# Moving an activation table load, two k and q requests and four value loads in a fused attention and feed-forward kernel

## The chip, the cores and the metric

The kernel runs on one core of a Trainium2 chip. The metric is the device time of one execution in microseconds: the median of 3 runs before the change is 313.27 us (313.2 to 313.47).

The core has five engines with instruction streams of their own. PE (TensorE) multiplies matrices into PSUM. ACT (ScalarE) evaluates functions (exp, ln, silu) from a table that must be loaded, and copies. DVE (VectorE) does elementwise work and 32x32 transposes. POOL (GpSimd) does elementwise work and issues DMAs through a queue of its own ("software_dynamic", q0); its DMAs can convert fp32 to bf16 on the way. SP (SyncE) only issues DMAs ("hardware_dynamic", q1), without conversion. All DMAs share the same 16 DMA engines. An engine runs its instructions in the order in which they were written and waits at semaphores.

## The reference

Two steps. First attention over q, k, v of shape 8 batches x 8 heads x 576 positions x 64, in fp32, as the sum of two parts:

```
q_d, k_d, v_d = means over groups of 4 neighbouring positions      # 144 positions
out_up    = each row of softmax(q_d k_d^T / 8) v_d, repeated 4 times
out_local = softmax(q k^T / 8 where |i - j| < 4) v
x = out_up + out_local, as 4608 tokens x 512
```

Then a feed-forward part on all tokens: `h = x @ w_in` (512 to 2048), `g = h * sigmoid(1.702 h)`, `out = g @ w_out` (2048 to 512), in fp32.

## The kernel before, in words

**Groups and batches.** The feed-forward part goes in nine groups g of 512 tokens. Group g has `mm1` (L831: 16 blocks ffc of 128 hidden columns, each with four matmuls of L816 over the 512 inputs, then one silu on ACT, L827, into `gT`) and `mm2` (L857: 64 matmuls of L894 that read `gT` and `w_out_bf`, then four output copies `osb` on ACT, L879, and four stores on SP, L884). Batch 0's attention runs ahead of everything. The attention of batch b = g + 1 is woven into group g: the lists `POS` and `POS_0` (L923) name matmul counts at which a piece of `attention(b)` is put into PE's stream. In group 0 the pieces for batch 1 are two scores pieces (16 and 28; their exponentials at 18), four pieces `avx1`, one for each pair of heads (40, 49, 58, 67), and `prep_vd_pe(1)` at 36 (L388), which forms the means of batch 1's values on PE from `vb`.

**What one piece needs.** k and q of a batch come by `load_qk` (L218, POOL, bf16) in two halves qd, and are transposed on DVE (L311) into `kT`, `qT`. The sums over four positions are `kdT`, `qdT` (L330 on DVE, or L342 and L346 on POOL). The values come in five chunks of 128 rows, in two halves of 64 partitions each: for batch 1 by POOL's DMAs straight into the bf16 tile `vb` (`load_vb`, L249, ten DMAs); for later batches by SP's DMAs into the fp32 tile `vf` (`load_v`, L238, ten DMAs), which POOL then casts into `vb` (`prep_v`, L352). The means of the values for batches from 2 on come from a second fp32 copy `v4` (`load_v4`, L271, SP), which POOL sums in three steps kc (`prep_v4`, L359 and L362) into `vd`.

**avx1** (L597, batch 1) and **avx** (L671, later batches) multiply the exponentials with the values on PE. ACT takes ln of the sums and exp(-ln) (L638, L649), DVE copies and multiplies (L643, L656) into `xT`, and POOL or, for the last pair, DVE adds the upsampled part (L667). After the last pair's exponential L653 loads the silu table again, and the output copies of group 0 follow on ACT.

**Order of the requests.** The order is written by hand (`manual_schedule`). At the start POOL issues k and q of batch 0 (L218), five value loads (L259), three loads of `w_in_bf` (L281), k and q of batch 1, and quarters 1 and 2 of `w_out_bf` (L290). In the loop for g = 0 (L1044) come ten `load_vb` for batch 1, quarters 3 and 4 of `w_out_bf`, the preparation of batch 1's k and q on DVE with the requests for batch 2's, a memset of `v4` (L1055) and `load_v(2)`. POOL has eight DMA semaphores that it uses in turn, so each of its DMAs waits until the one eight places before it has landed. `load_v(b, gate)` takes an optional gate: a copy of one element of another tile into element `[0, chunk 0]` of the `vf` tile (`after`, L928; L930 in the profile). SP's loads of batch 2 come behind such a copy from quarter 4 of `w_out_bf`. The tile `vf` has one buffer.

In the loop for g = 1 (b = 2) the order on POOL is: sums of k and q, `prep_v(2)`, `prep_v4(2)` with its three steps, then the four requests for batch 3's k and q.

Of the kernel before, what the change touches and what calls it, by code (L numbers as in the profile page):

```python
# [19 lines left out]
def kernel(  # L20
# [9 lines left out]
    nc = tc.nc  # L30
# [320 lines left out]
        cp = eng.copy if eng is nc.scalar else eng.tensor_copy  # L351
        cp(out=vbs[b % 2][:, i, h, 0:D], in_=vf[b][:, i, h])  # L352

    def prep_v4(b, eng):
        for kc in range(3):
            x = v4[0:112, kc].rearrange("p h (f d) -> p h f d", f=4)
            t1 = work.tile([128, SD * 4], FP32, name="pq", tag="pq")
            t1 = t1[:, 0 : HP * 2 * D].rearrange("p (h f d) -> p h f d", h=HP, f=2)
            eng.tensor_tensor(  # L359
                out=t1[0:112], in0=x[:, :, 0:2, :], in1=x[:, :, 2:4, :], op=ALU.add  # L360
            )
            eng.tensor_tensor(  # L362
                out=vds[b % 2][0:112, kc, :, 0:D],
                in0=t1[0:112, :, 0, :], in1=t1[0:112, :, 1, :], op=ALU.add,
            )
# [231 lines left out]
    def avx1(b, hp):  # L597
        vb, vd = vbs[b % 2], vds[b % 2]
        T, u, m, L, W = PB[1:3], hp % 2, hp // 2, 300, 300 + SD

        def down(kc, den):
            rows = slice(64 * u, 64 * u + 48)
            for j in range(2):
                nc.tensor.matmul(
                    T[u][64 * j : 64 * j + 64, den, L:W],
                    lhsT=ones[rows, 1, :] if den else vd[rows, kc, 2 * m + j, 0:D],
                    rhs=eds[m][rows, j, SD * kc : SD * kc + SD],
                    start=(kc == 0), stop=(kc == 2),
                    tile_position=(64 * u, 64 * j),
                )  # L610

        def local(par, i=None):
            rows = slice(64 * par, 64 * par + 64)
            at = slice(0, L) if i is None else slice(60 * i, 60 * i + 60)
            for j in range(2):
                nc.tensor.matmul(
                    T[par][64 * j : 64 * j + 64, int(i is None), at],
                    lhsT=ones[rows, 0, :] if i is None else vb[rows, i, 2 * hp + j, 0:D],
                    rhs=es[hp][rows, j, at],
                    start=True, stop=True,  # L620
                    tile_position=(64 * par, 64 * j),
                )

        others = [0, 1, 2, 3, 4, None]
        for kc in range(3):
            for den in range(2):
                down(kc, den)
                local(1 - u, others[2 * kc + den])
        for i in others:
            local(u, i)  # L630

        l = work.tile([128, 2 * (S + SD)], FP32, name="l", tag="l", bufs=2)
        n = work.tile([128, 2 * (S + SD)], FP32, name="n", tag="n", bufs=1)
        od = work.tile([128, 2, SD], FP32, name="od", tag="od", bufs=2)[:, 0]
        part = [slice(0, W), slice(W, W + L)]

        def ln(x):
            nc.scalar.activation(  # L638
                out=l[:, part[x]], in_=T[x ^ u][:, 1, 0 : (W, L)[x]], func=AF.Ln
            )  # L640

        def copy(x):
            nc.vector.tensor_copy(out=n[:, part[x]], in_=T[x ^ u][:, 0, 0 : (W, L)[x]])  # L643

        ln(0)
        copy(1)
        ln(1)
        copy(0)
        nc.scalar.activation(  # L649
            out=l[:, 0 : W + L], in_=l[:, 0 : W + L], func=AF.Exp, scale=-1.0  # L650
        )
        if hp == HP - 1:
            nc.scalar.preload_act_table_set("silu_and_others")  # L653

        def mult(out, *part):
            nc.vector.tensor_tensor(out=out, in0=sub(n, *part), in1=sub(l, *part), op=ALU.mult)  # L656

        x, t0 = xT[hp], b * S
        at = (0, W) if u == 0 else (W, 0)
        mult(od, L, (1, SD))  # L660
        mult(sub(x, t0 + 3, (114, 5), (1, 57)), at[0] + 3, (60, 5), (1, 57))
        mult(sub(x, t0 + 60, (114, 5), (1, 57)), at[1], (60, 5), (1, 57))
        mult(sub(x, t0, (1, 3)), at[0], (1, 3))
        mult(sub(x, t0 + 573, (1, 3)), at[1] + 297, (1, 3))
        xs = x[:, t0 : t0 + S].rearrange("p (t f) -> p t f", f=4)
        eng = nc.vector if hp == HP - 1 else nc.gpsimd
        eng.tensor_tensor(out=xs, in0=xs, in1=sub(od, 0, (1, SD), (0, 4)), op=ALU.add)  # L667
# [189 lines left out]
    def mm2(g, gT, steps):  # L857
        tok0 = g * TG
        turn["m"] = 1 if g else 2
        n = 0  # L860

        if g == 0:
            order = [(t0 + u, 4 * c + f)
                     for t0, c in ((0, 0), (0, 1), (2, 0), (2, 1),
                                   (0, 2), (2, 2), (0, 3), (2, 3))
                     for u in range(2) for f in range(4)]
        else:
            order = [(t, ffc) for t in range(4) for ffc in range(n_ffc)]
        ops = {}

        def store(t, ap, c0, n, eng, q):
            r0 = tok0 + 128 * t
            if g == 0 and t == 2:
                osb = work.tile([128, 2, S + SD], FP32, name="n", tag="n", bufs=1)
                osb = osb[:, 0, 0:n]
            else:
                osb = moe_sb.tile([128, n], FP32, name="osb", tag=f"osb{n}", bufs=3)
            if eng is nc.scalar:
                eng.activation(out=osb, in_=ap, func=AF.Copy, scale=1.0 / GELU_SCALE)  # L879
            else:  # L880
                eng.tensor_single_scalar(  # L881
                    out=osb, in_=ap, scalar=1.0 / GELU_SCALE, op=ALU.mult
                )
            q.dma_start(out=out[r0 : r0 + 128, c0 : c0 + n], in_=osb)  # L884

        for t, ffc in order:
            if g == n_groups - 1 and t == 3:
                continue
            for f in steps.get(n, ()):
                f()  # L890
            n += 1
            if ffc == 0:
                ops[t] = PB[0][:, t - 2, :] if g == 0 and t > 1 else pm_tile()
            nc.tensor.matmul(  # L894
                ops[t],
                lhsT=gT[:, ffc, t * 128 : (t + 1) * 128],
                rhs=w_out_bf[:, ffc, :],
                start=(ffc == 0), stop=(ffc == n_ffc - 1),
            )
            if ffc == n_ffc - 1 and not (g == 0 and t == 2):  # L900
                for u in (2, 3) if g == 0 and t == 3 else (t,):
                    store(u, ops[u], 0, d_model, nc.scalar, nc.sync)

        if g == n_groups - 1:
            for h in range(2):
                cols = slice(256 * h, 256 * h + 256)
                p = pm_tile()
                for ffc in range(n_ffc):
                    nc.tensor.matmul(  # L909
                        p[:, 0:256],  # L910
                        lhsT=gT[:, ffc, 384:512],
                        rhs=w_out_bf[:, ffc, cols],
                        start=(ffc == 0), stop=(ffc == n_ffc - 1),
                    )
                if h == 0:
                    store(3, p[:, 0:256], 0, 256, nc.scalar, nc.sync)
                else:
                    store(3, p[:, 0:128], 256, 128, nc.scalar, nc.scalar)
                    store(3, p[:, 128:256], 384, 128, nc.vector, nc.sync)
        for f in steps.get(n, ()):  # L920
            f()
# [120 lines left out]
    for g in range(n_groups):  # L1042
        b = g + 1
        if g == 0:  # L1044
            for i in range(5):
                load_vb(1, i)
            load_w_out(2)
            load_w_out(3)
            for qd in range(NQ):
                prep_qk(1, qd)  # L1050
                reduce_qk(1, qd, "k")
                reduce_qk(1, qd, "q")
                load_qk(2, qd)
# [3 lines left out]
        elif b < B:  # L1057
            load_v4(b)
            prep_qk(b, 0)
            pool_qk(b, 0)  # L1060
            if 2 < b < B - 1:
                for qd in range(NQ):
                    load_qk(b + 1, qd)
            prep_v(b, nc.gpsimd)
            if b + 1 < B:
                load_v(b + 1)
            prep_qk(b, 1)
            if b == 2:
                reduce_qk(b, 1, "k")
                reduce_qk(b, 1, "q")  # L1070
            else:
                pool_qk(b, 1)
            prep_v4(b, nc.gpsimd)
            if b == 2:
                for qd in range(NQ):
                    load_qk(b + 1, qd)
        steps = {}
        if b < B:
            for n, f in zip(POS if g else POS_0, attention(b)):
# [36 lines left out]
```

## Time and profile before

| | |
|---|---|
| median of 3 runs | 313.27 us (313.2 to 313.47) |
| profiled execution | 314.05 us |
| its span in the profile | 312.3 us |
| PE busy | 299.8 us, 96% |
| ACT busy | 203.4 us, 65% |
| DVE busy | 148.2 us, 47% |
| POOL busy | 147.2 us, 47% |
| POOL's DMA queue q0 | 18,784 packets, 14.95 MB |
| SP's DMA queue q1 | 45,072 packets, 24.32 MB |

How to read the profile. Times are microseconds from the start of the span. A line of the timeline gives start, length, engine, source line, operation, `out<-in`, sizes and a count, and in brackets the idle time just before it with what ended it. A line of the waits gives who waited for whom, the sum, how often, and the longest. A line of the DMA view gives what is loaded, the issuing queue, how many, KB each, and the median time from issue to landing. "PEclk" is the clock that PE was granted, in tenths of full speed, in 40 slices of the span. SPq is SP's instruction queue.

### The profile page before, as it was taken

The page shows a single profiled execution, that of the slowest core. Times are in us where ns is not written, and L with a number is a line of the kernel's source. Part 1 is how long each engine was busy: PE and PEld are TensorE (multiplying, and loading weights), DVE is VectorE, ACT ScalarE, POOL GpSimd, SP SyncE. Part 2 cuts the span into 40 slices and gives each one's busy share as a digit, 9 for nine tenths or more (in the row PEclk, how much of TensorE's full clock was granted, in tenths as well). Part 3 has the DMA queues.
Part 4 walks back from the last instruction along what each step waited for, and adds up shares of the span by engine and source line. Part 5 has one row for each costly group of instructions (what it writes and reads, how often), then busy time and mean ns, then how long its engine had stood idle before and what let it go on. Part 6 is the DMA issues. An engine that isn't in the chain of part 4 may idle for free.

```text
span 312.3 us, 9583 instructions
## 1 busy us (share of the span) xinstructions
PE 299.8 (96%) x4133; PEld 157.7 (51%) x4175; DVE 148.2 (47%) x303; ACT 203.4 (65%) x325; POOL 147.2 (47%) x169
## 2 busy tenths in 40 slices
PE   8899999999899999999999999999999999999995
PEld 3567554564544555455545554555454544444444
DVE  5983947851594049604980389028912760000000
ACT  4747765787767687668865895589568857316611
POOL 8552293287039933795359734983397110000000
PEclk9999999999999999999999999999999999999999
DMA  6999999877927941696169805981520110010011
GB/s 107 134 206 211 184 121 211 211 238 148 225 92 169 223 122 69 170 220 156 50 171 197 195 37 169 184 195 66 147 77 30 42 67 2 34 67 36 0 67 67
DMA packets 64042, 39.94 MB, mean 128 GB/s; under 512 B 44544, under 2 KB 54912, under 8 KB 64000
## 3 DMA queue, kind: packets, MB, share of 16 engines
q0 software_dynamic: 18784, 14.95, 32.7%
q1 hardware_dynamic: 45072, 24.32, 28.0%
q8 instruction: 32, 0.52, 0.7%
q10 hardware_dynamic: 144, 0.07, 0.1%
q14 instruction: 10, 0.08, 0.1%
HBM read 44.83 MB, written 9.44 MB: 174 GB/s over the span
## 4 chain that ended last, share of the span: by engine, by line
PE 79%; DMA 13%; ACT 2%; POOL 2%; issue 2%; DVE 1%; POOLq 0%; DVEq 0%; ACTq 0%
PE pm L894 34%; PE pm L816 22%; PE pa L816 13%; DMA w_out_bf<-in_moe_w_out_dram 9%; PE pa L439 3%; DMA vb<-in_v_dram 2%; PE pa L703 2%; PE pa L681 2%; DMA w_in_bf<-in_moe_w_in_dram 2%; PE pa L466 1%; PE pm L909 1%; ACT l L649 1%; POOL vb L249 1%; DVE xT L656 1%; ACT l L638 1%
## 5 line engine op out<-in xcount | busy, mean ns | idle before, releaser
L894 PE MATMUL pm<-w_out_bf,gT 128*128 128x512 bf16 x503 | 114.6, 379 | 3.8 <-issue 3.2
L816 PEld LDWEIGHTS <-w_in_bf 128*128 128x128 bf16 x627 | 60.7, 98 | 62.1 <-issue 0.9
L816 PE MATMUL pm<-xT,w_in_bf 128*128 128x512 bf16 (+1 forms) x351 | 86.8, 372 | 0.8 <-ACT osb L879 0.4
L894 PEld LDWEIGHTS <-gT 128*128 128x128 bf16 x560 | 52.8, 98 | 62.4 <-issue 0.6
L827 ACT ACTIVATE gT<-pm 128x512 bf16<-128x512 f32 x88 | 52.8, 604 | 38.8 <-PE pm L816 38.8
L816 PE MATMUL pa<-xT,w_in_bf 128*128 128x512 bf16 (+1 forms) x260 | 58.6, 347 | 0.4
L511 DVE TENSOR_TENSOR es<-es,mask 128x600 bf16<-128x600 bf16 x28 | 16.6, 626 | 85.8 <-ACT es L477 85.6
L879 ACT ACTIVATE osb<-pm 128x512 f32<-128x512 f32 (+2 forms) x35 | 20.3, 582 | 30.5 <-PE pm L894 25.1
L827 ACT ACTIVATE gT<-pa 128x512 bf16<-128x512 f32 x56 | 31.8, 611 | 7.8 <-PE pa L816 7.8
L773 POOL TENSOR_TENSOR xT<-xT,od 128x576 bf16<-128x576 bf16 x12 | 15.8, 1318 | 43.3 <-DVE xT L757 43.2
L757 DVE TENSOR_TENSOR xT<-n,l 128x285 bf16<-128x285 f32 (+1 forms) x96 | 28.1, 365 | 0.0
L342 POOL TENSOR_TENSOR pq<-kT 128x576 f32<-128x576 bf16 x11 | 12.8, 1160 | 30.4 <-DVE kT L311 30.4
L881 DVE TENSOR_SCALAR osb<-pm 128x128 f32<-128x128 f32 x1 | 0.3, 293 | 53.8 <-ACT osb L879 53.8
L359 POOL TENSOR_TENSOR pq<-v 112x512 f32<-112x512 f32 x18 | 23.7, 1315 | 0.7 <-DMA v<-in_v_dram 0.7
L311 DVE STREAM_TRANSPOSE kT<-kb 128x576 f32<-128x576 f32 x16 | 19.9, 1245 | 5.8 <-DMA kb<-in_k_dram 5.8
L311 DVE STREAM_TRANSPOSE qT<-qb 128x576 f32<-128x576 f32 x16 | 19.8, 1239 | 0.3 <-DMA qb<-in_q_dram 0.2
L503 ACT ACTIVATE ed<-pa 128x864 bf16<-128x864 f32 x16 | 14.3, 894 | 7.0 <-PE pa L466 7.0
L477 ACT ACTIVATE es<-pa 128x600 bf16<-128x600 f32 x28 | 17.2, 670 | 0.1
L752 ACT ACTIVATE l<-l 128x1440 f32<-128x1440 f32 x12 | 16.8, 1404 | 0.4
L747 DVE COPY n<-pa 128x492 f32<-128x492 f32 x24 | 15.0, 665 | 2.5 <-ACT l L746 1.9
L746 ACT ACTIVATE l<-pa 128x492 f32<-128x492 f32 x24 | 12.6, 578 | 5.0 <-PE pa L703 4.6
L439 PE MATMUL pa<-qT,kT 32*64 32x60 bf16 x1120 | 15.2, 195 | 0.0
(133 smaller groups left out, 355.7 us busy)
## 6 DMA issues: line engine op xcount, KB each, us to landing
out_dram<-osb SPq DMA_DIRECT2D x34, 256.0 KB, 2.0
vf<-in_v_dram SPq DMA_DIRECT2D x60, 128.0 KB, 4.4
v<-in_v_dram SPq DMA_DIRECT2D x72, 96.0 KB, 3.0
kb<-in_k_dram POOLq DMA_DIRECT2D x16, 288.0 KB, 6.6
qb<-in_q_dram POOLq DMA_DIRECT2D x16, 288.0 KB, 8.3
w_out_bf<-in_moe_w_out_dram POOLq DMA_DIRECT2D x4, 512.0 KB, 13.5
w_in_bf<-in_moe_w_in_dram POOLq DMA_DIRECT2D x2, 512.0 KB, 6.6
w_in_bf<-in_moe_w_in_dram POOLq DMA_DIRECT2D x1, 1024.0 KB, 12.5
```

The costliest lines, as they stand in the source:

```text
L311: nc.vector.transpose(out=t32.rearrange("p (i c) -> p c i", c=18), in_=store[b, qd].bitcast(FP32).rearrange("p (c d) -> p c d", c=18),)
L359: eng.tensor_tensor(out=t1[0:112], in0=x[:, :, 0:2, :], in1=x[:, :, 2:4, :], op=ALU.add)
L439: nc.tensor.matmul(P[1 + r // 2][64 * par : 64 * par + 64, r % 2, 60 * i : 60 * i + 60], lhsT=kT[b, qd][rows, k0 : k0 + 64, a], rhs=qT[b, ...
L477: nc.scalar.activation(out=es[2 * qd + u][:, :, 0:300], in_=sp[u][:, :, 0:300], func=AF.Exp, scale=inv_sqrt_d,)
L511: nc.vector.tensor_tensor(out=ev, in0=ev, in1=mask, op=ALU.mult)
L752: nc.scalar.activation(out=l, in_=l, func=AF.Exp, scale=-1.0)
L757: nc.vector.tensor_tensor(out=out, in0=sub(n, *part), in1=sub(l, *part), op=ALU.mult)
L773: eng.tensor_tensor(out=xs, in0=xs, in1=sub(od[:, u, :], 0, (1, SD), (0, 4)), op=ALU.add)
L816: nc.tensor.matmul(acc[:, c : c + n], lhsT=w_in_bf[:, dmc, ffc * 128 : (ffc + 1) * 128], rhs=xT[dmc][:, g * TG + c : g * TG + c + n], star ...
L827: nc.scalar.activation(out=gT[:, ffc, :], in_=acc, func=AF.Silu, scale=GELU_SCALE)
L879: eng.activation(out=osb, in_=ap, func=AF.Copy, scale=1.0 / GELU_SCALE)
L894: nc.tensor.matmul(ops[t], lhsT=gT[:, ffc, t * 128 : (t + 1) * 128], rhs=w_out_bf[:, ffc, :], start=(ffc == 0), stop=(ffc == n_ffc - 1),)
```

## The change

Three edits:

1. The silu table of group 0 is loaded behind the output copies of t = 0 and t = 1 in `mm2`, and no longer behind the last exponential in `avx1`.
2. `prep_v4` takes a list of steps. In group 1, step 0 of batch 2's value sums comes first, then the four requests for batch 3's k and q, then steps 1 and 2.
3. Of batch 1's values only chunks 0 to 2 are loaded by POOL as bf16. Chunks 3 and 4 are loaded by SP as fp32 into a `vf` tile (with a gate copy from quarter 1 of `w_out_bf`), and POOL casts them after it has issued quarters 3 and 4 of `w_out_bf`.

```
-    def prep_v4(b, eng):
-        for kc in range(3):
+    def prep_v4(b, eng, kcs=range(3)):
+        for kc in kcs:
...
-        if hp == HP - 1:
-            nc.scalar.preload_act_table_set("silu_and_others")
...
             if ffc == n_ffc - 1 and not (g == 0 and t == 2):
                 for u in (2, 3) if g == 0 and t == 3 else (t,):
                     store(u, ops[u], 0, d_model, nc.scalar, nc.sync)
+                if g == 0 and t == 1:
+                    nc.scalar.preload_act_table_set("silu_and_others")
...
         if g == 0:
-            for i in range(5):
+            for i in range(3):
                 load_vb(1, i)
+            load_v(1, gate=after(w_out_bf[0:1, 0, 0:1], nc.gpsimd), chunks=(3, 4))
             load_w_out(2)
             load_w_out(3)
+            prep_v(1, nc.gpsimd, slice(3, 5))
...
-            prep_v4(b, nc.gpsimd)
+            prep_v4(b, nc.gpsimd, (0,))
             if b == 2:
                 for qd in range(NQ):
                     load_qk(b + 1, qd)
+            prep_v4(b, nc.gpsimd, (1, 2))
```

## The prediction, made before the changed kernel was run

> **What bounds the kernel now.** I read the page first, then PE's waits, then the timelines of POOL, ACT and DVE around each wait, then the DMA view in short windows.
>
> ```profile
> span 312.3 us, 9583 instructions
> ...
> PE 299.8 (96%) x4133; PEld 157.7 (51%) x4175; DVE 148.2 (47%) x303; ACT 203.4 (65%) x325; POOL 147.2 (47%) x169
> ...
> PEclk9999999999999999999999999999999999999999
> ```
>
> PE is busy 96% of the span at an undisturbed clock, so only PE's idle moments can be won, and any work that keeps PE from starting is lost in full. PE's waits, longest first:
>
> ```profile
> PE pm L780 <- DVE wz L126: 1.2, 1, 1.2
> PE pa L423 <- DVE qT L311: 0.7, 1, 0.7
> ...
> PE pm L816 <- ACT osb L879: 0.4, 1, 0.4
> PE pm L894 <- DMA w_out_bf<-in_moe_w_out_dram: 0.4, 1, 0.4
> ```
>
> The last two are the only ones in which PE stands for something that this change touches late in the kernel. The L423 wait belongs to the start, and there the change has a side effect. From 92 us on, groups repeat every 32.4 us with PE full; what is won or lost before simply shifts them.
>
> **The w_out stall (0.37 us, at 48.28).** POOL issues batch 1's ten value loads ahead of the third quarter of w_out:
>
> ```profile
> 33.09 0.68 POOL L249 DMA_DIRECT2D vb<-in_v_dram  x1 [0.71 <-DMA qb<-in_q_dram]
> 35.73 0.68 POOL L249 DMA_DIRECT2D vb<-in_v_dram  x1 [1.97 <-DMA w_out_bf<-in_moe_w_out_dram]
> 38.94 2.07 POOL L249 DMA_DIRECT2D vb<-in_v_dram  x3 [2.53 <-DMA w_out_bf<-in_moe_w_out_dram]
> 40.99 1.53 POOL L290 DMA_DIRECT2D w_out_bf<-in_moe_w_out_dram  x2
> ```
>
> Each load waits for the one eight places before it. The change drops the last four value loads (4 x 0.68 = 2.7 us of issuing) and puts in one 1x1 copy (0.18, as L944), which waits for quarter 1, as the load at 35.73 did. So quarter 3 goes out at about 35.9 instead of 40.99, and quarter 4 at 38.94, once quarter 2 is in (38.66). Landing of quarter 3, an estimate: quarter 2 at 38.66, then the six value loads queued ahead (3,072 packets; the windows from 37 to 39 us move 1,100 per us: 2.8), then 3.2 for a quarter (35.45 to 38.66): 44.7. PE asks at 47.9. The stall goes, with 3 us to spare. **-0.37.**
>
> Added on POOL behind quarter 4's issue: the cast of two chunks, 1024/2560 of L352's 2.32 = 0.93, done at about 40.7; L388 reads it at 43.35. Behind it stand batch 2's k, q issues, the memset (2.65) and the second gate copy, all earlier than now since 2.7 went and 1.1 came. If that cover of 2.7 us were gone, PE would wait for the cast at L388.
>
> **The osb stall (0.40 us, at 60.20).**
>
> ```profile
> 57.42 0.82 ACT L649 ACTIVATE l<-l 128x744 f32<-128x744 f32 x1
> 58.26 1.28 ACT L653 ACT_TABLE_LOAD   x1
> 59.55 1.08 ACT L879 ACTIVATE osb<-pm 128x512 f32<-128x512 f32 x2
> ```
>
> PE was ready for the bank at 59.80 and got it when the first copy ended. With the table load behind the two copies, the first ends at 58.9. The work on ACT is the same: load and four copies end at 61.62 either way, and the first silu waited 0.96 for PE, so 0.77 less leaves it unharmed. No further load is needed: L879 runs between exponentials in later groups (77.48) at 0.62 without one. What is late next: xT of the last head pair (L667, ends 60.31), which PE would reach at 60.8 instead of 61.55; its chain also moves up with the first stall. **-0.40.** Together -0.77, and this is the ceiling.
>
> **Batch 3's q, k requests** (4 x 0.56) move from 74.32 to about 70.3, past two of the three value sums. These end at about 76.6 instead of 74.4; L681 first reads them at 80.4. Batch 3's transposes at 92.80 waited for nothing, nor did the cast at 99.94 that reads the value loads now run beside. **0**, behind 3 us of cover.
>
> **The four SyncE loads: not held where the code seems to hold them.** The gate copies w_out into chunk 0 of the tile, while the loads fill chunks 3 and 4. In the compiled order of the changed program SP's first four instructions are these loads, with no wait on them. SP has nothing else to do, so they go out when SP is released at 0.7 us, before POOL's first load (1.24), in the stretch in which DVE, and behind it PE and ACT, stand for k and q of batch 0:
>
> ```profile
> 5.61 1.26 DVE L311 STREAM_TRANSPOSE kT<-kb 128x576 f32<-128x576 f32 x1 [1.69 <-DMA kb<-in_k_dram]
> 7.04 1.25 DVE L311 STREAM_TRANSPOSE qT<-qb 128x576 f32<-128x576 f32 x1 [0.17 <-DMA qb<-in_q_dram]
> ```
>
> DVE then runs without a pause to 15.3, and PE waits on it (0.7, 0.6), so what q's landing slips, everything slips. Call it d. The trace of before has no SP traffic at the start; the nearest rows are k, q landing times here and where SP's loads run beside them. First the start, then batch 3 (beside ten vf loads); columns: KB, us from issue to landing.
>
> ```profile
> kb<-in_k_dram POOLq DMA_DIRECT2D x1, 288.0 KB, 4.3
> qb<-in_q_dram POOLq DMA_DIRECT2D x1, 288.0 KB, 5.1
> ```
>
> ```profile
> kb<-in_k_dram POOLq DMA_DIRECT2D x1, 288.0 KB, 5.6
> qb<-in_q_dram POOLq DMA_DIRECT2D x1, 288.0 KB, 6.6
> vf<-in_v_dram SPq DMA_DIRECT2D x2, 128.0 KB, 10.2
> ```
>
> q lands 1.5 later beside vf; in batch 4, beside the tail of the value-sum loads, the same view gives 4.7 and 5.8: 0.7 later. Here are four loads, not ten, and the first runs ahead of k. I take d = 1.0, just under the middle of 0.7 and 1.5. Bounds: below, 0 (they drain in gaps of the start; a gain is excluded, since nothing is taken away there). Above: all served ahead of q. In the window 69.4 to 75.6, vf alone moved 0.94 MB at 63.7% of the engines, 3.9 us of their full time; four loads of 0.128 MB take 2.2, less one load that runs ahead (0.55): 1.7.
>
> Later POOL transfers slip about as much as PE. The tightest is w_out's quarter 2: landed 38.66, first read at about 39.28; PE would stall again only if its slip exceeded d by 0.6.
>
> **A rule against the row.** Of SP's loads issued at 51.01, while POOL's 2304-byte packets ran, the trace has the first packet at 54.2, 3.2 us later; at 69.41, with POOL's queue empty, it came after 1.4. So a queue in service is not interrupted at once: the extra 1.8 us are eight of POOL's packets (window 74.9 to 79.3: 207 packets, 64.8% of 16 x 4.4 us, 0.22 each). [...]
>
> [...]
>
> **Sum.** The profiled execution took 314.05 us around a span of 312.3; the median of the runs shown is 313.27. Differences of the span are put on the median: 313.27 - 0.37 - 0.40 + 1.0 = 313.5.
>
> **Cases and chances.** A measurement can tell about 0.2% (0.63 us) from no change.
> - Forecast, 0.33: d between 0.8 and 1.4, 313.3 to 313.9. For it: the landing rows. Against: ten loads there, four here.
> - Turns, 0.22: d of 0.3 to 0.7, 312.8 to 313.2. For it: the late first packets after 51.01. Against: k itself landed 1.3 later in batch 3.
> - Hidden, 0.17: d under 0.14, about 312.5, both stalls gone and the loads free or held after all. For it: k, q use the engines with gaps at 6 to 7 us. Against: q was already 0.17 late for DVE.
> - Slower, 0.28: the loads, issued first, are served first; d from 1.4 to 1.7, at most 2.2: 313.9 to 314.7, typically 314.2. It decides from d = 1.40. For it: +1.5 in batch 3, k's early slot lost to a queue that starts 0.5 us earlier. Against: one load's head start, gaps at 6 to 7.
>
> Faster by over 0.2%: 0.17; within: 0.22 and nearly all of the forecast, 0.53; slower: 0.30. Range 312.6 to 314.4: it leaves out the best end of hidden and the worst of slower.
>
> **What would show it.** In the changed profile: SP busy from 0.7 us with four vf loads; DVE's first kT transpose later than 5.61 and qT later than 7.04 by about 1.0, and PE's L423 wait longer by as much; w_out issued near 36 + d; no w_out wait and no osb wait in PE's list; the first two osb copies directly behind the last L649. Wrong would be: qT on time (d counted for nothing), a wait of L894 for w_out's quarter 2 near 40, of L388 for POOL's cast near 43, or of L681 for the value sums near 80.

## The result, and the profile after

The changed kernel takes 314.9 us (median of 15 runs, 313.76 to 315.68). The kernel before, run beside it, takes 313.73 (15 runs, 313.2 to 314.95). The ratio is 1.003 with a 95% interval of 1.0017 to 1.0042: **slower by 0.94 us (0.53 to 1.32)**. (The two medians lie 1.17 apart, the two means 0.93; the ratio goes with the means.) The forecast was 313.5, its range ended at 314.4, and the side it held likeliest was "within 0.2%". The profiled execution took 314.96 us around this span (from the page):

```profile
span 313.2 us, 9630 instructions
...
PE 303.4 (97%) x4175; PEld 157.6 (50%) x4175; DVE 149.5 (48%) x303; ACT 203.5 (65%) x325; POOL 145.6 (47%) x167
```

PE's busy time cannot be set against the 299.8 of before: that trace has 42 matmul records fewer. (The list of before's waits is headed by 3.2 us in which L894 waits for "issue"; these are 20 gaps of 0.16 that stand in every trace with 4,133 records and in none with 4,175.) So I compare the same instruction on ACT or DVE in both traces ("shift", after minus before). Lines 654 to 902 of the kernel before stand two lower in kernels with edit 1 (L894 is L892 there). PE's waits in the changed kernel, longest first:

```profile
PE pa L423 <- DVE qT L311: 2.9, 1, 2.9
PE pm L778 <- DVE wz L126: 1.2, 1, 1.2
PE pm L423 <- DVE qT L311: 0.6, 1, 0.6
PE pm L388 <- DMA vb<-in_v_dram: 0.5, 1, 0.5
PE pa L388 <- issue: 0.5, 1, 0.5
```

Both waits that the change aimed at (w_out at L894, osb at L816) are gone from the list. Two new ones stand there, both in L388: one for batch 0's values at 16.4 us, one at 45.6 us that waits for nothing the profile shows. The 2.9 at L423 is not the slip of q: the second trace of before (experiment 9) has 1.8 there although its qT comes only 0.23 later than in the first, because the matmuls ahead of that wait end up to 0.85 earlier. The slip is read from DVE's qT.

**The start.** SP's timeline in the first 4 us, then DVE's:

```profile
0.74 2.89 SPq L238 DMA_DIRECT2D vf<-in_v_dram  x4
```

```profile
5.71 1.26 DVE L311 STREAM_TRANSPOSE kT<-kb 128x576 f32<-128x576 f32 x1 [1.79 <-DMA kb<-in_k_dram]
8.43 1.26 DVE L311 STREAM_TRANSPOSE qT<-qb 128x576 f32<-128x576 f32 x1 [1.46 <-DMA qb<-in_q_dram]
```

The four loads do go out at 0.74, unheld. kT is 0.10 later than before, qT 1.39. Why k is spared and q is not shows in the DMA view, first from 3.0 to 4.5 us, then from 8 to 10 (queue: packets, MB, share of 16 engines):

```profile
q0 software_dynamic: 104, 0.24, 97.8%
q1 hardware_dynamic: 36, 0.01, 2.4%
```

```profile
q0 software_dynamic: 166, 0.35, 90.7%
q1 hardware_dynamic: 277, 0.07, 21.5%
```

SP's queue (q1) ran alone until POOL's first packets came at 2.8 us; then k's burst had the engines (97.8%) and q1 nearly stopped (2.4%). From 4.5 to 8.0 us, with POOL's queue at 73.0%, q1 went on (33.1%), and by the packet records it sent its last piece only at 12.8 us, so it also ran beside batch 0's own value loads (from 10 us). POOL's gate copy on one of these loads stood at 12.93 before:

```profile
14.96 0.18 POOL L944 COPY gate<-vb 1x1 bf16<-1x1 bf16 x1 [5.57 <-DMA vb<-in_v_dram]
```

That is 2.03 later, against q's 1.39. PE followed q and so met the values too early: the 0.5 wait of L388. ACT's copy of the means (L396) shifts by 1.95.

**The middle.** POOL's timeline around quarters 3 and 4 of w_out:

```profile
37.37 0.17 POOL L930 CAST vf<-w_out_bf 1x1 f32<-1x1 bf16 x1 [1.60 <-DMA w_out_bf<-in_moe_w_out_dram]
37.49 0.77 POOL L290 DMA_DIRECT2D w_out_bf<-in_moe_w_out_dram  x1
40.71 0.74 POOL L290 DMA_DIRECT2D w_out_bf<-in_moe_w_out_dram  x1 [2.45 <-DMA w_out_bf<-in_moe_w_out_dram]
41.45 1.05 POOL L352 CAST vb<-vf 128x1024 bf16<-128x1024 f32 x1
```

Quarter 3 goes out 3.5 us earlier, as meant, and the cast ends at 42.50. PE's timeline at L388, which reads it:

```profile
45.30 0.30 PE L388 MATMUL pa<-vb,psel 128*64 128x256 bf16 x2
46.08 0.86 PE L388 MATMUL pa<-vb,psel 128*64 128x256 bf16 x12 [0.48 <-issue]
```

The cast was done 2.8 us before L388 began. Yet PE stopped after two matmuls, and the shift grew to 2.62. At 49.48 it is 2.08, since before stood here for w_out.

**The osb copies.** ACT's timeline:

```profile
58.97 0.82 ACT L649 ACTIVATE l<-l 128x744 f32<-128x744 f32 x1
59.70 1.06 ACT L877 ACTIVATE osb<-pm 128x512 f32<-128x512 f32 x2
60.78 1.28 ACT L902 ACT_TABLE_LOAD   x1
```

The two copies follow the last L649 at once, the load comes behind them, and the shift falls to 1.56. But this fall is not edit 1's. PE was ready for the bank at 61.84. With the load in its old place the first copy would have ended at 61.69, an estimate from the end of the last L649 (59.79), 1.28 for the load and 0.62 for the copy, and PE would not have waited either. In before, POOL could add for the first head pair only when quarter 4 had landed (50.8), and then ran beside DVE's multiplication into `od`, which took 1.10 instead of 0.31; that made ACT late for the osb copies. In the changed kernel quarter 4 landed at 48.2 and `od` took 0.31.

After 85 us the shift is 1.08, because the first trace of before has a pause of 0.34 at 84.39 (PE, L681) that the changed kernel lacks.

So the sum in this pair is 1.39 (q) + 0.56 (values) + 0.67 (L388) - 0.54 (w_out) - 0.52 (osb) - 0.48 (the pause at 84, less small rises before it) = about 1.1.

### The profile page after: what moved, and what is told of

Same layout as the page of the kernel before. It is cut to its first block, busy times and chain, and to the rows that moved or that the text cites. A ratio compares the mean times of both kernels' runs of the same rounds, so it can differ in the third digit from the quotient of the medians.

```text
span 313.2 us, 9630 instructions
## 1 busy us (share of the span) xinstructions
PE 303.4 (97%) x4175; PEld 157.6 (50%) x4175; DVE 149.5 (48%) x303; ACT 203.5 (65%) x325; POOL 145.6 (47%) x167
## 4 chain that ended last, share of the span: by engine, by line
PE 92%; DMA 3%; POOL 2%; issue 1%; DVE 1%; ACT 1%; POOLq 0%; DVEq 0%; ACTq 0%
PE pm L892 37%; PE pm L814 24%; PE pa L814 15%; DMA vb<-in_v_dram 3%; PE pa L439 3%; PE pa L892 2%; PE pa L701 2%; PE pa L679 2%; PE pa L466 2%; PE pm L909 1%; PE pa L575 1%; POOL vb L259 1%; PE pa L616 1%; PE pa L604 0%; POOL kb L218 0%
## 5 line engine op out<-in xcount | busy, mean ns | idle before, releaser
L892 PE MATMUL pm<-w_out_bf,gT 128*128 128x512 bf16 x528 | 119.4, 379 | 0.0
L814 PE MATMUL pm<-xT,w_in_bf 128*128 128x512 bf16 (+1 forms) x364 | 88.5, 372 | 0.0
L892 PEld LDWEIGHTS <-gT 128*128 128x128 bf16 x560 | 52.8, 98 | 62.4 <-issue 0.6
L511 DVE TENSOR_TENSOR es<-es,mask 128x600 bf16<-128x600 bf16 x28 | 17.8, 674 | 82.7 <-ACT es L477 82.6
L342 POOL TENSOR_TENSOR pq<-kT 128x576 f32<-128x576 bf16 x11 | 12.8, 1159 | 30.4 <-DVE kT L311 25.1
```

The lines of the kernel that those rows point to most:

```text
L511: nc.vector.tensor_tensor(out=ev, in0=ev, in1=mask, op=ALU.mult)
L814: nc.tensor.matmul(acc[:, c : c + n], lhsT=w_in_bf[:, dmc, ffc * 128 : (ffc + 1) * 128], rhs=xT[dmc][:, g * TG + c : g * TG + c + n], star ...
L892: nc.tensor.matmul(ops[t], lhsT=gT[:, ffc, t * 128 : (t + 1) * 128], rhs=w_out_bf[:, ffc, :], start=(ffc == 0), stop=(ffc == n_ffc - 1),)
```

## The experiments

Three theories stand in the expectations. **S**: the loss comes from the four value loads at the start. **M**: it comes from the middle, where POOL's cast or the values are late for L388. **F**: PE's own instructions come late. F arose because the DMA queue q8 ("instruction", 32 packets of 16 KB in an execution) has one of its packets close ahead of the pause in L388 (43.62 to 44.51 us in the changed kernel, by the packet records). Ratios are to runs of before taken beside each kernel, whose medians were 313.7 to 314.1.

**1. The loads really held.** The gate copy writes into the first chunk that is loaded, so that SP waits for quarter 1.

```
-            gate(t[0:1, 0, 0, 0:1])
+            gate(t[0:1, chunks[0], 0, 0:1])
```

> The changed kernel, but the gate copy goes into chunk 3, so that SP's four loads wait for w_out's quarter 1. Theory S (the loss is the loads at the start): qT starts at 7.0 again (8.43 in the changed kernel), L396 of batch 0 at 16.2 and not 18.1; the shift of 1.95 us goes, both stalls stay away, 1.2 to 1.9 us faster than before (312 against 313.7). Rival M (the loss is in the middle: POOL's cast holds up DVE's psel and PE's L388): the start is as before, but PE still loses 0.5 at L388 and the loads now meet w_out's quarter 2, so the time is within 0.5 us of before.

Measured: 320.37, ratio 1.0206 (1.0178 to 1.0235). The start is as before (qT at 6.95), so the gate explains the unheld loads. But the time is 6 us worse. PE's longest wait, then POOL's cast:

```profile
PE pa L388 <- POOL vb L352: 4.9, 1, 4.9
```

```profile
48.33 1.04 POOL L352 CAST vb<-vf 128x1024 bf16<-128x1024 f32 x1 [9.34 <-DMA vf<-in_v_dram]
```

SP issued from 35.5 on, and the loads landed 9.0 to 10.8 us after their issue, while POOL's queue carried w_out (quarters 3 and 4 issued at 35.40 and 38.25). The expected gain was a miss: holding the loads moves the price and multiplies it.

**2 to 4. Each edit alone.** Third: only the four lines in the loop for g = 0. First: only the table load. Second: only `prep_v4` in steps.

> Only the third edit (value chunks 3 and 4 by SP, not held). Theory S: +1.4 (q) +0.55 (batch 0's values) -0.4 (w_out) and about +0.5 near 45 us: 1.5 to 2.1 us slower than before. Rival M without the start: 0.5 slower at most, and the other two edits bring nothing.

> Only the first edit (table load behind two copies). Prediction's step: PE's wait of 0.40 for osb goes, 0.4 us faster. Rival: the next thing is late at the same place (xT of the last pair, or silu), under 0.1 us.

> Only the second edit (batch 3's q, k requests earlier). Theory F: in the kernel before, PE runs out of instructions near 84.4 us because its 16 KB instruction loads wait behind POOL's and SP's packets; the earlier requests take the crowd away from there: 0.3 to 0.7 us faster, and no PE gap at 84. Prediction's step: 0. Rival: the gap of before at 84 us is a gap in the records only, no change.

Measured: third 315.22, ratio 1.004 (1.0022 to 1.0058); first 313.6, 0.9991 (0.9972 to 1.001); second 313.24, 0.998 (0.996 to 0.9999). The loss lies in edit 3. With it alone qT starts at 8.74 and PE pauses in L388 again, 0.36 at 45.9. Without edit 1 it has no osb wait either, nor has the kernel with two loads below. With edit 1 alone the osb wait is gone and the silu behind it runs 0.47 earlier, but the interval includes no change. The second alone is at the edge of measurable.

**5 and 6. The loads without the rest.** Four, then two, SP loads that nobody reads, added to the kernel before.

```
             load_w_out(3)
+            load_v(1, chunks=(3, 4))     # second kernel: chunks=(3,)
```

> The kernel before, plus the four SP loads of value chunks 3 and 4 at the start, into a tile that nobody reads; all ten of POOL's value loads stay. Theory S: q of batch 0 lands about 1.4 us later, batch 0's values another 0.5, so L396 of batch 0 comes 1.9 to 2.3 us later and the time is 1.2 to 2.2 us above before. Rival M (the loss comes with the cast and the shorter POOL list): within 0.4 us of before.

> As the run with four unread loads, but two (chunk 3 only). If the loads cost what they move beside q (turns): the first runs ahead of k for nothing, the second costs about a third of the three that hurt: q 0.3 to 0.6 us later, batch 0's values about 0.9 later, time 0.4 to 1.0 us above before. If what costs is that SP's queue is in use at all, the same 1.4 as with four.

Measured: four 315.57, ratio 1.0058 (1.004 to 1.0076); two 314.33, 1.0037 (1.0016 to 1.0058). Loads that do nothing but run at the start are enough to lose as much as the change does: S. Two of them cost qT 0.80 in their trace and four cost it 0.79 in theirs, so one pair of traces does not separate the two cases; by the ratios two lose 0.5 to 1.8 us and four 1.3 to 2.4, and these overlap.

**7. Edits 1 and 2 without 3.** The diff is that of the change without the lines for g = 0.

> Edits 1 and 2 without 3. By the runs of each alone (0.3 and 0.65 us, both barely clear of nothing): 0.5 to 1.0 us faster than before. If the gap of before at 84 us is an accident of one execution: 0.3 faster, from edit 1 alone.

Measured: 312.75 against 313.79, ratio 0.998 (0.9962 to 0.9998). It is 0.6 us faster than the kernel before (0.06 to 1.2), though its profiled execution stood 1.2 us for w_out, 0.64 for quarter 2 and 0.60 for quarter 3:

```profile
PE pm L892 <- DMA w_out_bf<-in_moe_w_out_dram: 1.2, 2, 0.6
```

The wait that edit 3 was aimed at is the one for quarter 3. Seven traces have POOL's old order up to quarter 4. Three of them show it (0.37 and 0.32 in before, 0.60 here), and four do not (edit 1 alone, edit 2 alone, both kernels of 5 and 6). So this wait comes and goes with the landing of w_out, and only part of its absence can be put down to edit 3.

**8. The loads at 13 us.** Held by a copy behind L944, into chunk 3, ahead of the w_in load.

```
+    load_v(1, gate=after(gate, nc.gpsimd), chunks=(3, 4))
     load_w_in(0, 512)
```

> All three edits, but the four SP loads wait for batch 0's second value chunk (the copy at L944, about 13 us), when q0 has its gap between batch 0's values and w_in. Theory S: nothing is lost at the start; the loads land by 18 us, w_in about 1 us later with 2 us in hand; both stalls stay away, so 0.6 to 1.4 us faster than before. If w_out's quarter 2 becomes late: 0.2 to 0.5 less of it. Rival M: the loss in the middle stays, no faster than before.

Measured: 315.28, ratio 1.0055 (1.0037 to 1.0072), another miss. The start is unharmed (qT at 7.10), but now w_in and w_out come late:

```profile
PE pm L892 <- DMA w_out_bf<-in_moe_w_out_dram: 2.1, 2, 1.3
```

None of the three places tried is free for these 0.5 MB: with all three edits and the loads at 0.7, 13 and 35 us the kernel is slower than before by 0.9, 1.7 and 6.5 us.

**9 and 10. Both kernels profiled again**, unchanged.

> The kernel before, profiled a second time. If the 0.34 us pause of TensorE at 84.4 us in the first profile belongs to the order of the requests, it is there again between 84 and 85 us; if it is an accident of one execution (theory F: an instruction load of TensorE that came late), it is gone or elsewhere and the second half is 0.6 us earlier than in the first profile. The start should repeat: qT's transpose at 7.0 within 0.2, w_out's wait of L894 0.3 to 1.2.

> The changed kernel, profiled a second time. Theory S (the four loads at the start): qT's transpose again 0.8 to 1.7 later than before's, batch 0's means of the values (L396) later still by about 0.5. Theory F: a pause of TensorE inside L388 at 45 to 46 us again, 0.3 to 0.5; if it is an accident, it is gone.

Measured, one execution each: 313.95 and 314.47, spans 312.2 and 312.7. Two of before's waits repeat:

```profile
PE pm L816 <- ACT osb L879: 0.4, 1, 0.4
PE pm L894 <- DMA w_out_bf<-in_moe_w_out_dram: 0.3, 1, 0.3
```

The pause at 84 us is not in the list of waits, but it is there, smaller and at the same matmul: the group of four that took 0.23 in edit 2's trace takes 0.48. PE's timeline in before's second trace, then with edit 2 alone:

```profile
84.22 0.48 PE L681 MATMUL pa<-ed,vd 48*64 48x144 bf16 x4
84.46 0.31 PE L681 MATMUL pa<-ed,ones 48*64 48x144 bf16 x4
```

```profile
84.35 0.23 PE L681 MATMUL pa<-ed,vd 48*64 48x144 bf16 x4
84.41 0.23 PE L681 MATMUL pa<-ed,ones 48*64 48x144 bf16 x4
```

Counted over all 15 traces, the third matmul of this group starts late in three: 0.56 in before, 0.23 in its second trace, 0.53 with two loads. All three lack edit 2. In the six traces without edit 2 a q8 packet starts 25 to 27 matmuls ahead of it and ends 1.36 to 1.54 us before it starts, a distance like the one after which PE went on in L388 where it had stopped there (1.28 to 1.63, experiments 12 and 13); in the nine with edit 2 the packet starts 48 to 118 matmuls ahead and ends 2.2 us or more before. This fits theory F as it was expected for edit 2: the earlier requests let the packet through sooner. In the changed kernel qT comes at 7.63, so the loads cost 0.36 in this pair, not 1.39; but the pause in L388 is there again, and longer. PE's timeline:

```profile
44.33 0.30 PE L388 MATMUL pa<-vb,psel 128*64 128x256 bf16 x2
45.60 0.86 PE L388 MATMUL pa<-vb,psel 128*64 128x256 bf16 x12 [0.97 <-issue]
```

**11. No loads and no cast.** The changed kernel with zeros in the two chunks.

```
-            load_v(1, gate=after(w_out_bf[0:1, 0, 0:1], nc.gpsimd), chunks=(3, 4))
...
-            prep_v(1, nc.gpsimd, slice(3, 5))
+            nc.gpsimd.memset(vbs[1][:, 3:5, :, 0:D], 0.0)
```

> The changed kernel without the four SyncE loads and without their cast: the last two value chunks of batch 1 are left out and filled with zeros by a memset of POOL at the place of the cast, so part of batch 1's values is left out of the output. Theory S: everything that was lost is lost to these 0.5 MB. qT is back at 7.04 within 0.2, the w_out and osb waits stay gone, and the time is 0.8 to 1.4 below the kernel before (about 312.4 to 312.9) and about 2 below the changed kernel. Theory F: the pause of 0.3 to 0.5 at 45 to 46 us stays, since POOL's queue is again done early, and the gain on the kernel before is 0.3 to 0.5 less, 313.0 to 313.4.

Measured: 313.28 against 314.14, ratio 0.9974 (0.996 to 0.9988): 0.82 below before. qT is at 6.88, so S holds for the start. But PE still pauses, with no cast and no transfer of SP in the kernel at that time, which rules out the cast and SP's loads, and so M, as its cause:

```profile
43.10 0.30 PE L388 MATMUL pa<-vb,psel 128*64 128x256 bf16 x2
43.95 0.75 PE L388 MATMUL pa<-vb,psel 128*64 128x256 bf16 x10 [0.55 <-issue]
```

It eats all that the missing w_out wait brought (0.53 on ACT).

**12 and 13. POOL's pause put back.** The gate copy reads quarter 2 instead of quarter 1, in the changed kernel and in the one without chunks (there the copy goes into `vb`, ahead of the memset).

```
-            load_v(1, gate=after(w_out_bf[0:1, 0, 0:1], nc.gpsimd), chunks=(3, 4))
+            load_v(1, gate=after(w_out_bf[0:1, 4, 0:1], nc.gpsimd), chunks=(3, 4))
```

> The changed kernel with its gate copy from quarter 2 of w_out instead of quarter 1 (one index). POOL then waits at that copy until quarter 2 has landed, near 40 us, and issues quarters 3 and 4 some 2 to 3 us later than in the changed kernel, so its queue runs empty before them, as it did in the kernel before. Theory F (TensorE's instruction load is served only when POOL's queue pauses, and the new pause of TensorE inside L388 at 45 us is its price): the load moves from matmul 597 back to about matmul 490, the pause of 0.4 to 1.0 is gone, and since quarter 3 still lands ahead of its use (issue at about 40.8, 3.2 for a quarter, some 44 against 50), the time is 0.4 to 0.8 below the changed kernel, 0.0 to 0.5 above the kernel before. Rival C (the pause belongs to the cast by POOL or to the values' landing): it stays where it is, at matmul 600 to 607, or grows, since the cast also comes 2 us later.

> The kernel without the four loads and the cast (the last two value chunks of batch 1 are zeros, so part of batch 1's values is left out of the output), with a 1x1 copy from quarter 2 of w_out ahead of the issue of quarters 3 and 4. Same question without the loads at the start: by theory F the instruction load moves to about matmul 490, the pause of 0.55 at 43.4 goes, and the time falls from 0.86 to 1.2 to 1.6 below the kernel before (312.2 to 312.9). By rival C nothing at 43 us changes and the time stays 0.7 to 1.0 below.

Where q8's packet falls is read in the DMA view. In the kernel before, 39.4 to 41.2 us:

```profile
q0 software_dynamic: 1011, 0.12, 155.8%
q8 instruction: 1, 0.02, 5.3%
```

In the changed kernel there is none from 41.2 to 43.4, and one in the window behind it, 43.4 to 44.6:

```profile
q0 software_dynamic: 598, 0.36, 185.0%
```

```profile
q0 software_dynamic: 242, 0.24, 119.2%
q8 instruction: 1, 0.02, 4.7%
```

With the gate on quarter 2, POOL's timeline and, from 41.2 to 43.4 us, the DMA view:

```profile
40.01 0.18 POOL L930 CAST vf<-w_out_bf 1x1 f32<-1x1 bf16 x1 [4.30 <-DMA w_out_bf<-in_moe_w_out_dram]
40.24 1.51 POOL L290 DMA_DIRECT2D w_out_bf<-in_moe_w_out_dram  x2
```

```profile
q0 software_dynamic: 480, 0.24, 129.7%
q8 instruction: 1, 0.02, 4.5%
```

The same window that held no instruction load now holds one. PE's timeline of L388, with the loads and then without chunks:

```profile
45.23 0.97 PE L388 MATMUL pa<-vb,psel 128*64 128x256 bf16 x14
```

```profile
43.20 0.97 PE L388 MATMUL pa<-vb,psel 128*64 128x256 bf16 x14
```

All 14 matmuls run in one piece in both: **F**, and not C. Over all 15 traces the picture is the same. Where the packet starts by the 493rd matmul, the third matmul of L388 follows without a stop, and it starts 1.98 us or more after the packet's end. (With edit 2 alone PE stops ten matmuls later, 0.34 for the values.) Where it starts at the 597th or later (the change, its second profile, edit 3 alone, the held loads, no chunks), PE stops at the third matmul, for 0.15 us with the held loads and 0.36 to 0.97 in the others, and goes on 1.28 to 1.63 after the packet's end.

The times: 314.24 against 313.69, ratio 1.0021 (1.0005 to 1.0036), and 312.77, ratio 0.997 (0.9958 to 0.9982). Of the first, the expected place just above before holds in the main (0.55 above). The second should have reached 1.2 to 1.6 below before and reached 0.92. Against the kernels without the gate on quarter 2 the intervals overlap, so F's 0.4 to 0.8 is shown by the traces, not by the clock.

## Why the prediction was wrong

| term | predicted | measured |
|---|---|---|
| w_out stall | -0.37 | -0.53 on ACT against before's first trace; no stall in four of seven traces with the old order |
| osb stall | -0.40 | -0.52, but not by edit 1 |
| q late by d | +1.0 | +1.19 (0.6 to 1.7) |
| values of batch 0 | 0 | +0.49 |
| L388 at 45 us | 0 | +0.59 (0.36 to 0.97) |
| edit 2 | 0 | -0.23 to -0.56 in three of six traces without it, 0 in three; alone -0.63 by the clock (-1.26 to -0.03) |
| sum | +0.23 | +1.22 without edit 2; by the clock +0.94 (0.53 to 1.32) |

The forecast of 313.5 was 0.23 above a median of 313.27, and the kernel before came out at 313.73 beside the change. Of the distance from 313.5 to 314.9, 0.46 is this and the rest is in the terms. That the terms come near the clock is partly luck, since three of them scatter by half a microsecond from trace to trace.

- **The loads are unheld, at 0.7 us:** right, and undone by one index in experiment 1.
- **d = 1.0:** right in size. qT starts at 7.63 to 8.74 in the five profiles with four loads (mean 8.21) and at 6.88 to 7.27 in the nine without loads at the start (7.02). One pair of traces would have given 0.36 or 1.39. The case "slower" was tied to d from 1.40, and it came about at a smaller d.
- **Turns (0.22, d of 0.3 to 0.7):** no run shows the term behind this d, queues that are served in turns of a fixed number of packets, and the measured d of 1.19 lies above its range. What the traces showed in its place: k was 0.10 late though SP's queue was first, and q 1.39, while SP's queue moved 0.23 MB beside k and q from 4.5 to 8.0 us.
- **"Later POOL transfers slip about as much as PE":** this step failed. The loads ran on to 12.8 us, so batch 0's own values slipped more than q. L396 starts at 17.17 to 18.46 with the loads (mean 17.85) and at 15.93 to 16.48 without (16.17): 1.68, which is 0.49 over d. The prediction watched w_out's quarter 2 as the tightest transfer; it was the values.
- **"The stall goes, with 3 us to spare":** the stall went, quarter 3 was issued at 37.49 as forecast (36 + d). What failed, as the second step, is what would be late next. The prediction named POOL's cast, which had 2.8 us in hand. It did not count q8's packet, which started at 39.57 us in before, ahead of quarter 3's issue at 40.99, and at 43.62 in the changed kernel, behind quarter 3's at 37.49. The gain became a new wait of the same size.
- **The osb stall** behaved as worked out with edit 1 alone, the first silu included. In the changed kernel ACT came early for the copies anyway, since edit 3 had brought quarter 4 sooner. The prediction added up the two terms ("Together -0.77") as if they were independent; both hang on when w_out lands.
- **Edit 2 at 0:** the prediction looked at what reads the value sums and batch 3's k and q, which was indeed on time, and left out what else their packets delay. Alone edit 2 is faster by an interval that ends 0.03 short of no change, and the traces show what it can remove: the late start at 84 us. How much of it a usual execution has stays open.

Also open: which rule makes q8's packet wait. Without chunks but with the pause, it was served at 38.48 us among hundreds of value packets, so a busy queue alone does not hold it back. Its lateness goes with the packets of w_out: from PE's 484th matmul to the start of q8's packet, 348 to 456 of them started in the five traces in which it is late, and at most 30 in the ten others.

## What to carry to other kernels

A transfer taken off a full queue is not free on another: here two queues divided the same 16 engines (POOL's 97.8% and SP's 2.4% from 3.0 to 4.5 us of the changed kernel, 73.0% and 33.1% from 4.5 to 8.0), so ask which landing each moved byte will delay, for all requests until the moved ones have drained, and not only for the first. A pause in a DMA queue may be in use: q8's packet started at 39.57 us with POOL's pause in before, and at 43.62 without it in the changed kernel. Look at q8 before you close one. Read a gate for the region that it writes: with the copy in chunk 0 the loads of chunks 3 and 4 went out at 0.74 us, and with it in chunk 3 at 35.5. And before a pause of 0.3 us is counted for or against anything, take a second profile and look for the same instruction: it may be late by less, and below what the list of waits shows.

## What the runs showed of the hardware

- **PE paused behind late packets of q8.** This queue ("instruction") moved 0.52 MB in 32 packets of 16 KB in an execution, 125 of PE's matmuls apart on average (packet records of before). Most went by without a pause: in the changed kernel's list of waits "issue" stands once, with 0.5 us. One late packet cost PE 0.15 to 0.97 us, in four kernels at the same matmul, and another 0.23 to 0.56 us in two kernels. That the packets are PE's own instructions is theory F, which rests on this pace and on experiments 12 and 13. The profile calls the pause "issue", or, where it is short, shows only a longer group.
- **Two groups of DVE instructions took longer beside a POOL operation.** The four L207 operations took 1.51 us before and 2.46 in the changed kernel, where the cast of 1.05 ran beside them. With POOL idle in most of that stretch (the held loads) they took 1.16. The L656 multiplication into `od` took 1.10 before, where POOL added beside it (1.20, from 50.95), and 0.31 in the changed kernel where POOL was not adding.
- **SP's value loads landed late beside w_out:** 9.0 to 10.8 us after issue in experiment 1, for 0.5 MB, while POOL's queue carried w_out. The median of the 60 such loads in before is 4.4.
